# A fused chunk-selecting attention and ELU MLP on one core: selection moved to a [chunk, query] layout, persistent mask tiles, half-batch MLP with the ELU over three engines

## The chip, the cores and the metric

The kernel runs on one core of one Trainium2 chip. The metric is the device time of one execution in microseconds (us), as the median of several runs. Lower is better.

## The reference, cut to what matters

```python
# q, k, v: [4 batches, 8 heads, 768 positions, 64]; chunks of 32 keys, 24 chunks a head
k_min = np.min(k_chunks, axis=3); k_max = np.max(k_chunks, axis=3)
ub = np.sum(np.maximum(q*k_min, q*k_max), axis=-1)       # bound of each query against each chunk
ub = np.where(causal, ub, -1e9)
top_chunks = np.argsort(ub, axis=-1)[..., -6:]           # the 6 best chunks of each query
mask = sel & (pos[:, None] >= pos[None, :])
attn = softmax(where(mask, q @ k.T / 8, -1e9))           # shortened
x = (attn @ v) transposed to [3072 tokens, 512]          # shortened
h = x @ w_in                                             # w_in [512, 2048]
g = np.where(h > 0.0, h, np.exp(np.minimum(h, 0.0)) - 1.0)   # ELU
return g @ w_out                                         # w_out [2048, 512]
```

The work is done by head pairs: 4 batches with 4 pairs each give 16 pairs, called 0 to 15. A batch's MLP can start when its four pairs are done. The mask does not appear as a separate step in the score matmul: 24 extra rows of the stationary operand hold -40000 where a key belongs to a chunk, and 24 extra rows of the moving operand hold 1 where the query did *not* select that chunk. The score matmul of a pair therefore cannot start until its selection is known.

## The kernel before

Both weight matrices are asked for on the GpSimd queue as the last item of the set-up. For each pair, ScalarE copies the transposed queries out of PSUM, VectorE builds the operands, TensorE computes the bound in [query, chunk] layout, VectorE finds the sixth largest, TensorE transposes the selection, and VectorE copies it into the operand.

```python
psT = ... bufs=4, PSUM   # transposes, bounds
psS = ... bufs=3, PSUM   # scores and, under another name (psM = psS), all MLP results
psO = ... bufs=1, PSUM
# ... constants by GpSimd ...
w_in_sb = wpool.tile([P, DMODEL // P, DFF], BF16, name="w_in_sb")
nc.gpsimd.dma_start(out=w_in_sb, in_=moe_w_in.rearrange("(k p) f -> p k f", p=P))
w_out_sb = wpool.tile([P, DFF // P, DMODEL], BF16, name="w_out_sb")
nc.gpsimd.dma_start(out=w_out_sb, in_=moe_w_out.rearrange("(k p) f -> p k f", p=P))
# ...
# phase_b1, set-up of a pair
        nc.vector.tensor_copy(out=lhsA[64:P, :], in_=econst[64:P, :])      # three constant blocks
        nc.vector.tensor_copy(out=lhsB[0:64, :], in_=econst[0:64, :])      # copied anew for every pair
        nc.vector.tensor_copy(out=rhsA[64:P, :], in_=zconst[64:P, :])
        # ... q transposed by TensorE; 8 ScalarE copies of it, two of them Abs ...
        # ... k transposed; ScalarE copies it to KTf ...
        nc.vector.tensor_copy(out=lhsA[0:64, :], in_=KTf[0:64, :])
        nc.vector.tensor_copy(out=lhsB[64:128, :], in_=KTf[64:128, :])
        nc.vector.tensor_copy(out=vext[:, :, :, 0:D], in_=v_pair)
        # ... kmid = kmax + kmin, krad = kmax - kmin, per head block ...
# phase_b2, the bound of 128 queries at a time against 2 x 24 chunks, in fp32
        for qi, qt in enumerate(range(1, NQT)):
            nc.tensor.matmul(ub_ps[:, qi, :], lhsT=QTf[:, 128 * qt:128 * (qt + 1)], rhs=kmidBD,
                             start=True, stop=False)
            nc.tensor.matmul(ub_ps[:, qi, :], lhsT=absQTf[:, 128 * qt:128 * (qt + 1)], rhs=kradBD,
                             start=False, stop=True)
        # ... top six, comparison, 6 transposes of the selection ...
        nc.vector.tensor_copy(out=rhsB[0:64, 0:512], in_=selps0[0:64, :])
        nc.vector.tensor_copy(out=rhsA[64:88, 0:512], in_=selps0[64:88, :])
        # ...
# phase_d, MLP of a batch: 16 blocks of 128 hidden units x 768 tokens
            for hw, tc0, tw in ((hw0, 0, 512), (hw1, 512, 256)):
                nc.scalar.activation(out=e_sb[:, 0:tw], in_=hw, func=AF.Exp)
                nc.vector.tensor_scalar(out=t_sb[:, 0:tw], in0=e_sb[:, 0:tw], scalar1=1.0,
                                        scalar2=1.0, op0=AOT.min, op1=AOT.subtract)
                nc.vector.tensor_tensor(out=gT[:, fc, tc0:tc0 + tw], in0=t_sb[:, 0:tw],
                                        in1=hw, op=AOT.max)
```

The softmax here doesn't subtract the row's maximum and nothing guards it: scores larger than these inputs give would overflow.

Of the kernel before, what the change touches and what calls it, by code (L numbers as in the profile page):

```python
# [9 lines left out]
AOT = mybir.AluOpType  # L11
AF = mybir.ActivationFunctionType
F32 = mybir.dt.float32
# [10 lines left out]
NTOK = B * S  # L24
# [3 lines left out]
NQT = S // P  # L28
MASKNEG = -40000.0
CAUSNEG = -1.0e9  # L30

NPAIR = H // 2


@with_exitstack
def kernel(
# [8 lines left out]
    dev_pairs=None,  # L45
    dev_mlp=None,
    dev_dump=None,
# [3 lines left out]
    const = ctx.enter_context(tc.tile_pool(name="const", bufs=1))  # L51
    wpool = ctx.enter_context(tc.tile_pool(name="wpool", bufs=1))
    xtpool = ctx.enter_context(tc.tile_pool(name="xtpool", bufs=8))
    gtpool = ctx.enter_context(tc.tile_pool(name="gtpool", bufs=1))
    ldpool = ctx.enter_context(tc.tile_pool(name="ldpool", bufs=3))
    tspool = ctx.enter_context(tc.tile_pool(name="tspool", bufs=3))
    bigpool = ctx.enter_context(tc.tile_pool(name="bigpool", bufs=4))
    smpool = ctx.enter_context(tc.tile_pool(name="smpool", bufs=3))
    selpool = ctx.enter_context(tc.tile_pool(name="selpool", bufs=4))
    ptpool = ctx.enter_context(tc.tile_pool(name="ptpool", bufs=18))  # L60
    opool = ctx.enter_context(tc.tile_pool(name="opool", bufs=3))
    mlppool = ctx.enter_context(tc.tile_pool(name="mlppool", bufs=2))
    psT = ctx.enter_context(tc.tile_pool(name="psT", bufs=4, space=bass.MemoryType.PSUM))
    psS = ctx.enter_context(tc.tile_pool(name="psS", bufs=3, space=bass.MemoryType.PSUM))
    psO = ctx.enter_context(tc.tile_pool(name="psO", bufs=1, space=bass.MemoryType.PSUM))
    psM = psS
# [6 lines left out]
    nc.gpsimd.tensor_copy(out=ident_b, in_=ident_f)  # L73

    tri01 = const.tile([P, P], BF16, name="tri01")
    tri_tmp = const.tile([P, P], F32, name="tri_tmp")
    nc.gpsimd.memset(tri_tmp, 1.0)
    nc.gpsimd.affine_select(out=tri_tmp, in_=tri_tmp, compare_op=AOT.is_ge,
                            fill=0.0, base=0, pattern=[[1, P]], channel_multiplier=-1)
    nc.gpsimd.tensor_copy(out=tri01, in_=tri_tmp)  # L80

    e24_tmp = const.tile([P, S], F32, name="e24_tmp")
    nc.gpsimd.memset(e24_tmp, MASKNEG)
    for r0, cnt in ((0, 64), (64, 64)):
        nc.gpsimd.affine_select(out=e24_tmp[r0:r0 + cnt], in_=e24_tmp[r0:r0 + cnt],
                                compare_op=AOT.is_ge, fill=0.0, base=0,
                                pattern=[[1, S]], channel_multiplier=-32)
        nc.gpsimd.affine_select(out=e24_tmp[r0:r0 + cnt], in_=e24_tmp[r0:r0 + cnt],
                                compare_op=AOT.is_ge, fill=0.0, base=31,
                                pattern=[[-1, S]], channel_multiplier=32)  # L90
    econst = const.tile([P, S], BF16, name="econst")
    nc.gpsimd.tensor_copy(out=econst, in_=e24_tmp)
    zconst = const.tile([P, S], BF16, name="zconst")
    nc.gpsimd.memset(zconst, 0.0)

    causal_sel = const.tile([P, NQT, 2, NCH], F32, name="causal_sel")
    nc.gpsimd.memset(causal_sel, 0.0)
    for j in range(4):
        nc.gpsimd.affine_select(out=causal_sel[32 * j:32 * (j + 1)],
                                in_=causal_sel[32 * j:32 * (j + 1)],  # L100
                                compare_op=AOT.is_ge, fill=CAUSNEG, base=j,
                                pattern=[[4, NQT], [0, 2], [-1, NCH]], channel_multiplier=0)

    w_in_sb = wpool.tile([P, DMODEL // P, DFF], BF16, name="w_in_sb")
    nc.gpsimd.dma_start(out=w_in_sb, in_=moe_w_in.rearrange("(k p) f -> p k f", p=P))
    w_out_sb = wpool.tile([P, DFF // P, DMODEL], BF16, name="w_out_sb")
    nc.gpsimd.dma_start(out=w_out_sb, in_=moe_w_out.rearrange("(k p) f -> p k f", p=P))

    pairs = [(b, r) for b in range(B) for r in range(NPAIR)]
    if dev_pairs is not None:  # L110
        pairs = dev_pairs
    mlp_batches = list(range(B))
    if dev_mlp is not None:
        mlp_batches = dev_mlp

    xT = {}

    def phase_a(b, r):
        q_pair = ldpool.tile([P, NQT, 2, D], F32, name="q_pair")
        k_pair = ldpool.tile([P, NQT, 2, D], F32, name="k_pair")  # L120
        v_pair = ldpool.tile([P, NQT, 2, D], F32, name="v_pair")
        for hidx in range(2):
            hh = 2 * r + hidx
            nc.sync.dma_start(out=q_pair[:, :, hidx, :],
                              in_=q[b, hh].rearrange("(n p) d -> p n d", p=P))
            nc.sync.dma_start(out=k_pair[:, :, hidx, :],
                              in_=k[b, hh].rearrange("(n p) d -> p n d", p=P))
            nc.sync.dma_start(out=v_pair[:, :, hidx, :],
                              in_=v[b, hh].rearrange("(n p) d -> p n d", p=P))
        return (q_pair, k_pair, v_pair)  # L130

    def phase_b1(b, r, lds, resd):
        q_pair, k_pair, v_pair = lds
        lhsA = bigpool.tile([P, S], BF16, name="lhsA")
        lhsB = bigpool.tile([P, S], BF16, name="lhsB")
        rhsA = bigpool.tile([P, S], BF16, name="rhsA")
        rhsB = bigpool.tile([P, S], BF16, name="rhsB")
        nc.vector.tensor_copy(out=lhsA[64:P, :], in_=econst[64:P, :])
        nc.vector.tensor_copy(out=lhsB[0:64, :], in_=econst[0:64, :])
        nc.vector.tensor_copy(out=rhsA[64:P, :], in_=zconst[64:P, :])  # L140
        psQ0 = psT.tile([P, 512], F32, name="psQ0", tag="ps")
        psQ1 = psT.tile([P, 256], F32, name="psQ1", tag="ps")
        for n in range(NQT):
            src_q = q_pair[:, n, :, :]
            if n < 4:
                nc.tensor.transpose(psQ0[:, 128 * n:128 * (n + 1)], src_q, ident_f)
            else:
                nc.tensor.transpose(psQ1[:, 128 * (n - 4):128 * (n - 3)], src_q, ident_f)
        QTf = tspool.tile([P, S], F32, name="QTf")
        nc.scalar.activation(out=QTf[:, 0:512], in_=psQ0, func=AF.Copy, scale=0.5)  # L150
        nc.scalar.activation(out=QTf[:, 512:768], in_=psQ1, func=AF.Copy, scale=0.5)
        nc.scalar.activation(out=rhsA[0:64, 0:512], in_=psQ0[0:64, :], func=AF.Copy)
        nc.scalar.activation(out=rhsB[64:128, 0:512], in_=psQ0[64:128, :], func=AF.Copy)
        nc.scalar.activation(out=rhsA[0:64, 512:768], in_=psQ1[0:64, :], func=AF.Copy)
        nc.scalar.activation(out=rhsB[64:128, 512:768], in_=psQ1[64:128, :], func=AF.Copy)
        absQTf = tspool.tile([P, S], F32, name="absQTf")
        nc.scalar.activation(out=absQTf[:, 0:512], in_=psQ0, func=AF.Abs, scale=0.5)
        nc.scalar.activation(out=absQTf[:, 512:768], in_=psQ1, func=AF.Abs, scale=0.5)
        yield

        psK0 = psT.tile([P, 512], F32, name="psK0", tag="ps")
        psK1 = psT.tile([P, 256], F32, name="psK1", tag="ps")
        for n in range(NQT):
            src_k = k_pair[:, n, :, :]
            if n < 4:
                nc.tensor.transpose(psK0[:, 128 * n:128 * (n + 1)], src_k, ident_f)
            else:
                nc.tensor.transpose(psK1[:, 128 * (n - 4):128 * (n - 3)], src_k, ident_f)
        KTf = tspool.tile([P, S], F32, name="KTf")
        nc.scalar.activation(out=KTf[:, 0:512], in_=psK0, func=AF.Copy)  # L170
        nc.scalar.activation(out=KTf[:, 512:768], in_=psK1, func=AF.Copy)
        nc.vector.tensor_copy(out=lhsA[0:64, :], in_=KTf[0:64, :])  # L172
        nc.vector.tensor_copy(out=lhsB[64:128, :], in_=KTf[64:128, :])  # L173
        vext = selpool.tile([P, NQT, 2, D + 1], BF16, name="vext")
        nc.gpsimd.memset(vext[:, :, :, D:D + 1], 1.0)
        nc.vector.tensor_copy(out=vext[:, :, :, 0:D], in_=v_pair)  # L176
        kv = KTf[:, :].rearrange("p (c w) -> p c w", c=NCH)
# [18 lines left out]
                         rhsB=rhsB, vext=vext, kmidBD=kmidBD, kradBD=kradBD))  # L196

    def phase_b2(b, r, st):
        QTf = st["QTf"]
        absQTf = st["absQTf"]  # L200
        kmidBD = st["kmidBD"]
        kradBD = st["kradBD"]
# [257 lines left out]
```

## Time and profile before

| | before |
|---|---|
| time, median (lowest to highest of 3 runs) | 464.08 us (463.63 to 464.13) |
| span of the profiled run, mean granted TensorE clock | 461.3 us, 0.941 |
| first softmax exp | 51.3 us |
| pairs 0 to 3 (little else runs), first exp to the end of pair 3 | 57.7 us |

The page of the profile opens with the busy time of each engine, then cuts the span into 40 slices of 11.5 us; each digit is the busy share in tenths (the row of TensorE is shown), and PEclk is the clock that the throttle granted to TensorE.

```profile
span 461.3 us, 7376 instructions
PE 351.4 (76%) x2534; PEld 219.5 (48%) x2560; DVE 313.3 (68%) x1064; ACT 221.1 (48%) x513; POOL 26.4 (6%) x104
...
PE   3411986678569999778569999697478999878896
...
PEclk9999997798899999888899999977999999989999
```

No engine is full. In the first four slices (46 us) TensorE does 3, 4, 1 and 1 tenths. What ended its waits is listed by the view of waits (us in total, times, longest us):

```profile
PE h_ps L335 <- DVE gT L343: 22.9, 22, 3.5
PE sps L273 <- DVE rhsA L238: 21.7, 9, 3.3
PE selps_302 L236 <- DVE selv L227: 15.0, 1, 15.0
PE ub_ps L208 <- DVE kmidBD L188: 11.4, 2, 6.6
```

The four longest waits all end with VectorE: for the last ELU pass, which frees the MLP's PSUM buffer, for the mask rows that VectorE copies, and for the selection and its bound at the start. The timeline of the start (start us, us, engine, instruction) shows what VectorE itself stood behind:

```profile
10.81 0.93 POOL L105 DMA_DIRECT2D w_in_sb<-in_moe_w_in_dram  x1
...
11.74 1.29 POOL L107 DMA_DIRECT2D w_out_sb<-in_moe_w_out_dram  x1
...
12.47 9.45 SPq L128 DMA_DIRECT2D v_pair<-in_v_dram  x1
...
37.12 0.56 DVE L176 CAST vext<-v_pair 128x768 bf16<-128x768 f32 x1 [18.22 <-DMA v_pair<-in_v_dram]
...
51.30 1.08 ACT L276 ACTIVATE pt<-sps 128x512 bf16<-128x512 f32 x2 [6.51 <-PE sps L273]
```

The weights are asked for at 10.8 and 11.7 us. From then on the sync engine's issues stretch (9.45 us for one), and VectorE stands 18.2 us for one load of v. The first exp runs at 51.3 us.

In the MLP's first half alone, near the end, TensorE repeats a pattern; two blocks of 768 tokens lie between 429.25 and 432.81 us, 3.56 us for 2 x 3072 = 6144 columns:

```profile
429.25 0.60 PE L335 MATMUL h_ps<-xt,w_in_sb 128*128 128x256 bf16 x4 [0.31 <-DVE gT L343]
...
432.81 0.60 PE L335 MATMUL h_ps<-xt,w_in_sb 128*128 128x256 bf16 x4 [0.31 <-DVE gT L343]
```

The bound matmuls are fp32, and the trace records two passes for each: 160 matmuls leave 320 records. Eight passes lie between 63.95 and 64.85 us, about 0.11 us each:

```profile
63.95 0.39 PE L210 MATMUL ub_ps<-kradBD,absQTf 128*128 128x48 f32 x2
...
64.85 0.39 PE L210 MATMUL ub_ps<-kradBD,absQTf 128*128 128x48 f32 x2
```

### The profile page before, as it was taken

The numbers are of one execution on the slowest core, as the hardware profiler recorded it, in microseconds if no ns is written. First come the engines' busy times: TensorE is split into PE (matmuls) and PEld (weight loads), VectorE is DVE, ScalarE is ACT, GpSimd is POOL, SyncE is SP. The second block draws the span as 40 slices with busy tenths as digits, with TensorE's granted clock in tenths as the row PEclk, the third lists the DMA queues.
The fourth block names the chain that finished last, engine by engine and source line by source line (L and its number), as shares of the span: only waits on it lengthen the run. The fifth ranks groups of instructions, "written<-read, shape, count | busy, mean of one in ns | idle before, by whom it ended". The sixth has DMA issues, their size and how long they took to land.

```text
span 461.3 us, 7376 instructions
## 1 busy us (share of the span) xinstructions
PE 351.4 (76%) x2534; PEld 219.5 (48%) x2560; DVE 313.3 (68%) x1064; ACT 221.1 (48%) x513; POOL 26.4 (6%) x104
## 2 busy tenths in 40 slices
PE   3411986678569999778569999697478999878896
PEld 3301764556246445566236444575245644644442
DVE  3605688877958927877968916777968935769921
ACT  4303585576267207765267306773365505745500
POOL 9400000001000000000000000000000000000000
PEclk9999997798899999888899999977999999989999
DMA  9999342343003211442202211300000021000011
GB/s 219 213 195 257 90 96 64 89 102 85 19 2 69 58 68 48 104 102 59 47 1 68 59 68 47 70 1 1 0 1 1 2 86 52 2 0 1 0 70 68
DMA packets 81348, 29.83 MB, mean 65 GB/s; under 512 B 75680, under 2 KB 77728, under 8 KB 81312
## 3 DMA queue, kind: packets, MB, share of 16 engines
q1 hardware_dynamic: 78720, 25.17, 22.0%
q0 software_dynamic: 2592, 4.19, 5.0%
q8 instruction: 20, 0.33, 0.3%
q14 instruction: 16, 0.13, 0.1%
HBM read 27.26 MB, written 6.29 MB: 73 GB/s over the span
## 4 chain that ended last, share of the span: by engine, by line
PE 51%; DVE 30%; ACT 9%; issue 4%; SPq 4%; DMA 1%; DVEq 0%
PE mo_ps L349 18%; PE h_ps L333 8%; ACT pt L276 6%; PE sps L273 6%; DVE gT L343 5%; PE h_ps L335 5%; PE ub_ps L210 4%; PE ub_ps L208 4%; DVE t_sb L341 3%; PE o_ps L291 3%; ACT e_sb L339 3%; DVE kmax L180 3%; DVE kmin L181 2%; DVE lhsA L172 2%; DVE lhsB L173 1%
## 5 line engine op out<-in xcount | busy, mean ns | idle before, releaser
L276 ACT ACTIVATE pt<-sps 128x384 bf16<-128x384 f32 (+2 forms) x224 | 93.6, 508 | 113.2 <-PE sps L273 111.8
L339 ACT ACTIVATE e_sb<-h_ps 128x512 f32<-128x512 f32 (+1 forms) x128 | 61.1, 491 | 64.8 <-PE h_ps L333 35.5
L349 PE MATMUL mo_ps<-w_out_sb,gT 128*128 128x512 bf16 x376 | 83.1, 379 | 0.4
L333 PE MATMUL h_ps<-xt,w_in_sb 128*128 128x512 bf16 x238 | 71.8, 404 | 6.2 <-ACT pt L276 2.8
L343 DVE TENSOR_TENSOR gT<-t_sb,h_ps 128x512 bf16<-128x512 f32 (+1 forms) x128 | 66.7, 548 | 1.2
L335 PE MATMUL h_ps<-xt,w_in_sb 128*128 128x256 bf16 x256 | 46.1, 285 | 24.8 <-DVE gT L343 22.9
L273 PE MATMUL sps<-rhsA,lhsA 128*128 128x384 bf16 x144 | 41.7, 328 | 24.1 <-DVE rhsA L238 21.7
L349 PEld LDWEIGHTS <-gT 128*128 128x128 bf16 x384 | 37.6, 98 | 44.4
L341 DVE TENSOR_SCALAR t_sb<-e_sb 128x512 f32<-128x512 f32 (+1 forms) x128 | 43.7, 359 | 19.3 <-ACT e_sb L339 17.3
L352 DVE COPY o_sb<-mo_ps 128x512 f32<-128x512 f32 x24 | 16.6, 690 | 51.3 <-PE mo_ps L349 51.3
L273 PE MATMUL sps<-rhsB,lhsB 128*128 128x384 bf16 x144 | 41.2, 322 | 10.8 <-ACT pt L276 10.2
L335 PEld LDWEIGHTS <-w_in_sb 128*128 128x128 bf16 x256 | 25.9, 102 | 45.1 <-issue 38.5
L291 PEld LDWEIGHTS <-pt 128*128 128x128 bf16 x672 | 32.7, 107 | 22.9 <-DVE pt L280 14.3
L291 PE MATMUL o_ps<-vext,pt 128*128 128x65 bf16 x672 | 38.7, 207 | 3.3 <-DVE pt L280 2.8
L208 PE MATMUL ub_ps<-kmidBD,QTf 128*128 128x48 f32 x160 | 32.0, 284 | 11.4 <-DVE kmidBD L188 11.4
L333 PEld LDWEIGHTS <-w_in_sb 128*128 128x128 bf16 x256 | 25.9, 104 | 30.1 <-issue 16.2
L280 DVE TENSOR_TENSOR pt<-pt,tri_107 128x128 bf16<-128x128 bf16 x192 | 31.3, 220 | 5.1 <-ACT pt L276 3.8
L208 PEld LDWEIGHTS ub_ps<-kmidBD,QTf 128*128 128x128 f32 x160 | 27.2, 209 | 13.1 <-issue 12.2
L210 PE MATMUL ub_ps<-kradBD,absQTf 128*128 128x48 f32 x160 | 33.2, 291 | 0.0
L273 PEld LDWEIGHTS <-lhsA 128*128 128x128 bf16 x144 | 14.1, 106 | 35.8 <-DVE rhsA L238 23.8
L176 DVE CAST vext<-v_pair 128x768 bf16<-128x768 f32 x16 | 8.9, 558 | 28.4 <-DMA v_pair<-in_v_dram 28.2
L210 PEld LDWEIGHTS ub_ps<-kradBD,absQTf 128*128 128x128 f32 x160 | 26.7, 209 | 0.0
(538 smaller groups left out, 400.4 us busy)
## 6 DMA issues: line engine op xcount, KB each, us to landing
q_pair<-in_q_dram SPq DMA_DIRECT2D x32, 192.0 KB, 3.2
k_pair<-in_k_dram SPq DMA_DIRECT2D x32, 192.0 KB, 3.1
v_pair<-in_v_dram SPq DMA_DIRECT2D x32, 192.0 KB, 3.2
out_dram<-o_sb SPq DMA_DIRECT2D x24, 256.0 KB, 2.0
w_in_sb<-in_moe_w_in_dram POOLq DMA_DIRECT2D x1, 2048.0 KB, 14.0
w_out_sb<-in_moe_w_out_dram POOLq DMA_DIRECT2D x1, 2048.0 KB, 26.4
```

The source lines that it names most:

```text
L208: nc.tensor.matmul(ub_ps[:, qi, :], lhsT=QTf[:, 128 * qt:128 * (qt + 1)], rhs=kmidBD, start=True, stop=False)
L210: nc.tensor.matmul(ub_ps[:, qi, :], lhsT=absQTf[:, 128 * qt:128 * (qt + 1)], rhs=kradBD, start=False, stop=True)
L273: nc.tensor.matmul(sps[:, pc:pc + w], lhsT=lhs_of[hd][:, 128 * kb:128 * (kb + 1)], rhs=rhs_of[hd][:, c0:c0 + w], start=True, stop=True)
L276: nc.scalar.activation(out=pt[:, 0:wtot], in_=sps[:, 0:wtot], func=AF.Exp, scale=SCALE)
L280: nc.vector.tensor_tensor(out=pt[:, pc:pc + 128], in0=pt[:, pc:pc + 128], in1=tri01, op=AOT.mult)
L291: nc.tensor.matmul(o3_ps[:, hd, qi, :], lhsT=pt[:, off:off + 128], rhs=vext[:, kb, hd, :], start=(kb == 0), stop=(kb == qt))
L333: nc.tensor.matmul(hw0, lhsT=wblk, rhs=xT[(b, kk)][:, 0:512], start=(kk == 0), stop=(kk == DMODEL // P - 1))
L335: nc.tensor.matmul(hw1, lhsT=wblk, rhs=xT[(b, kk)][:, 512:768], start=(kk == 0), stop=(kk == DMODEL // P - 1))
L339: nc.scalar.activation(out=e_sb[:, 0:tw], in_=hw, func=AF.Exp)
L341: nc.vector.tensor_scalar(out=t_sb[:, 0:tw], in0=e_sb[:, 0:tw], scalar1=1.0, scalar2=1.0, op0=AOT.min, op1=AOT.subtract)
L343: nc.vector.tensor_tensor(out=gT[:, fc, tc0:tc0 + tw], in0=t_sb[:, 0:tw], in1=hw, op=AOT.max)
L349: nc.tensor.matmul(o_ps, lhsT=gT[:, fc, 128 * tt:128 * (tt + 1)], rhs=w_out_sb[:, fc, :], start=(fc == 0), stop=(fc == DFF // P - 1))
```

## The change

The intent: take VectorE, which ended the longest waits, out of the way of TensorE. The bound is computed transposed, with the chunks as the stationary side and 288 queries moving, two pairs side by side in the two column halves of the array. Its formula changes with it: instead of q and |q| against the middle and the width of a chunk's range, it is q against the chunk's minimum plus max(q, 0), called Qrl in the traces, against maximum less minimum. The first 192 queries see at most six chunks and are left out, so 576 queries remain. VectorE's 32x32 block transpose turns it for the top-six search and back, and four small DMAs put the selection into the operands of two pairs; no TensorE transpose and no VectorE copy remains. The constant blocks are written once into four persistent sets. The MLP works on half batches of 384 tokens, and its middle ELU pass goes to GpSimd. Loads of q and k are issued before the set-up, and the weights after the first preparation. The core of the diff (the whole file is rewritten; cuts are marked by `...`, and the comments are added here):

```diff
-    psT = ctx.enter_context(tc.tile_pool(name="psT", bufs=4, space=bass.MemoryType.PSUM))
-    psS = ctx.enter_context(tc.tile_pool(name="psS", bufs=3, space=bass.MemoryType.PSUM))
-    psM = psS
+    psT = pool("psT", 2, space=bass.MemoryType.PSUM)
+    psS = pool("psS", 2, space=bass.MemoryType.PSUM)
+    psM = pool("psM", 3, space=bass.MemoryType.PSUM)
 ...
+    lds = {t: load(t) for t in range(2)}                  # q and k first, before the constants
 ...
+    for s in range(NSET):                                 # once, not per pair
+        nc.vector.tensor_copy(out=lhsA[s][64:P, :],
+                              in_=econst[64:P].rearrange("p c w -> p (c w)"))
 ...
+            nc.scalar.activation(out=lhsA[s][0:64, ts], in_=ps[0:64, :], func=AF.Copy)    # K
+            nc.scalar.activation(out=lhsB[s][64:P, ts], in_=ps[64:P, :], func=AF.Copy)
 ...
+    def select(g):                                        # for two pairs at once
+        for u in range(2):
+            ub = psT.tile([P, HQ], F32, name="ub", tag="ps")
+            for w in range(2):
+                for j in range(2):
+                    t = 2 * g + j
+                    nc.tensor.matmul(ub[64 * j:64 * j + 64, :], lhsT=kst[t % NSET][:, w, :],
+                                     rhs=qf[t][w][:, HQ * u:HQ * (u + 1)],
+                                     start=(w == 0), stop=(w == 1))
+            nc.vector.transpose(out=ubT[:, HB * u:HB * (u + 1), :].rearrange("p b c -> p (b c)"),
+                                in_=ub)
 ...
+        nc.vector.transpose(out=selT, in_=sb[:, :, :].rearrange("p b c -> p (b c)"))
+        for j in range(2):
+            s = (2 * g + j) % NSET
+            nc.sync.dma_start(out=rhsA[s][64:64 + NCH, Q0:S], in_=selT[64 * j:64 * j + NCH, :])
+            nc.sync.dma_start(out=rhsB[s][0:NCH, Q0:S], in_=selT[64 * j + 32:64 * j + 32 + NCH, :])
 ...
-                nc.vector.tensor_scalar(out=t_sb[:, 0:tw], in0=e_sb[:, 0:tw], scalar1=1.0,
-                                        scalar2=1.0, op0=AOT.min, op1=AOT.subtract)
-                nc.vector.tensor_tensor(out=gT[:, fc, tc0:tc0 + tw], in0=t_sb[:, 0:tw],
-                                        in1=hw, op=AOT.max)
+            nc.gpsimd.tensor_scalar(out=m_sb, in0=e_sb, scalar1=-1.0, scalar2=1.0,
+                                    op0=AOT.add, op1=AOT.mult)
+            nc.vector.scalar_tensor_tensor(out=gT[:, fc, :], in0=hw, scalar=0.0, in1=m_sb,
+                                           op0=AOT.max, op1=AOT.min)
 ...
+    prep_group(0)
+    load_w_in()
+    select(0)
+    prep_group(1)
+    load_w_out()
+    for g in range(ng):
+        attend(2 * g)
+        if g + 1 < ng:
+            select(g + 1)
+        attend(2 * g + 1)
+        if g + 2 < ng:
+            prep_group(g + 2)
+        if g % 2 == 1 and g >= 3:
+            for hf in range(2):
+                mlp((g - 3) // 2, hf)
```

## The prediction

> **What bounds the kernel now.** Span 461 us; no engine is full: TensorE 351 us (76%), VectorE 313 (68%), ScalarE 221 (48%), GpSimd 26 (the page's busy table). The chain of waits is 51% TensorE, 30% VectorE, 9% ScalarE. The stretches read:
> - Start: the first softmax exp runs near 49 us. TensorE is busy only 12 us in the first 46. Both weight matrices (8.4 MB at 215 GB/s) are asked for at 11 us; the SP queue's issues then stretch from 0.6 to 3-9 us, and pair 2's loads arrive late (timeline).
> - Attention alone (50-112 us): 15-16 us a pair. VectorE is 76-82% busy; the score matmuls wait 3.3 us a pair for the mask rows that VectorE copies into rhs; the granted clock falls to 0.73.
> - MLP, first half alone (425-437 us): 3.55 us per two blocks, where the matmuls need 2.6 at full clock: TensorE waits for ScalarE then two VectorE passes to free three PSUM buffers.
> - MLP, second half: 96 matmuls at 217 ns, 20.9 us a batch, pure TensorE. Untouched.
>
> **What changes, costed from the trace.**
> - ELU: the min/subtract pass (43.7 us VectorE) goes to GpSimd as 128 passes of 128x384. GpSimd's casts took 280 ns (128 wide) and 1030 (768): about 0.6 us each, 75 us total, an estimate. The last pass stays: 0.55 us x 128 = 70 us against 66.7.
> - Setup copies a pair (econst, zconst, lhs casts, vext, mask rows, block-diagonal builds): about 4 us of VectorE a pair disappear (persistent tiles, cast on the v DMA, ScalarE copies). The 192 triangle products become 64 larger ones. MAX8 only 160 -> 144.
> - Together VectorE falls from 313 to about 215 us. ScalarE stays near 225 (Q/absQ/KTf copies replaced by half-width ones).
> - TensorE: 320 fp32 bound matmuls at 110 ns (weight-load bound, 36 us) become 64 of 288 columns; 0.25-0.5 us each, 15-31 us. 96 selection transposes vanish (5 us). Hidden-layer matmuls 83 us either way. Pipelined work at full clock: about 309 -> 290 us. So TensorE hardly shrinks; what goes is its waiting.
> - Start: q/k first, weights after the first preps; attention should begin near 25 us, not 49. The mask now goes by four small DMAs on the SP queue behind loads.
>
> **Sum.** About 25 us start. Pairs 0-7 are mostly attention in the new instruction order: ScalarE 9.9 us a pair, TensorE 7.7 at full clock; say 12 us: 96 us, hiding some 11 us of MLP. Left: eight pairs and the MLPs, about 218 us TensorE at full clock; at 0.95 clock and 6% stalls 243. Tail 4. Total about 368; I say 370. TensorE should then be near 85% busy.
>
> The Trainium skill, "TensorE: Matmul & The Clock Gate", part 1, says idle TensorE windows lower its clock; this trace agrees (0.73 at 69-92 us, 1.00 when dense). Denser work should raise the mean above 0.941. "GPSIMD Engine Reference", section 1, says GpSimd shares SBUF interfaces with VectorE and contends with two-SBUF-input or two-port passes; no number here shows it.
>
> **What would show each step.** GpSimd m_sb mean near 0.6 us; VectorE total 205-230; first exp by 25-28 us; bound-matmul pitch under 0.5 us; MLP-only blocks near 0.8 us (three PSUM buffers, chain 2.4 us); mean clock at or over 0.95; last MLP's second half unchanged at 10.4 us per half-batch.
>
> **What would make it wrong.** GpSimd passes over 1 us, lengthening the PSUM release; v DMAs waiting in GpSimd's in-order queue ahead of ELU passes; mask DMAs held behind loads at each group; only two score and two transpose PSUM buffers (three and four before) starving the attention stage; ScalarE, unrelieved, pacing longer than assumed. Better: fp32 bound matmuls run in parallel column halves, stalls vanish: 345.

## More of the kernel before

The page counts time before the first clock record as full clock; in this trace the records begin only at 56.1 us, so the first four digits of PEclk and most of the fifth are not measured.

## The result

| | before | after |
|---|---|---|
| time, median (lowest to highest of 4 runs) | 464.11 us (463.63 to 465.49) | 396.31 us (395.87 to 396.63) |
| ratio, 95% interval | | 0.852 (0.850 to 0.855) |
| profiled span, mean clock as printed | 461.3 us, 0.941 | 394.6 us, 0.930 |
| first softmax exp | 51.3 us | 49.6 us |
| first exp to the end of pair 3 | 57.7 us | 52.5 us |
| first exp to the end of the span | 410.0 us | 344.9 us |

A ratio is the mean time of one kernel's runs over that of the other's runs of the same rounds, so it is not quite the ratio of the medians that are quoted. An unchanged copy of the kernel after, run later, gave 396.16 us and 0.852 again.

The page of the kernel after, the same lines:

```profile
span 394.6 us, 6477 instructions
PE 317.5 (80%) x2272; PEld 175.1 (44%) x2272; DVE 205.0 (52%) x594; ACT 226.5 (57%) x489; POOL 116.2 (29%) x244
...
PE   1562068678869869999998788999999988979886
...
PEclk9995559959998989999999699999999999999999
```

VectorE fell from 313.3 to 205.0 us. TensorE fell from 351.4 to 317.5 us and is busier (80%). Its idle time, span less busy time, fell from 109.9 to 77.1 us. So of the 66.7 us of span, 33.9 us are work that TensorE no longer does, and 32.8 us are waiting that is gone. In the first 49 us its idle time hardly moved (34.2 us before, 33.1 after). After those 49 us it was 75.8 us before and is 44.0 after. So almost the whole gain lies after the start. The waits of TensorE, after:

```profile
PE sps L243 <- DMA rhsA_119<-selT: 15.4, 1, 15.4
PE h_ps L295 <- DVE gT L303: 11.5, 28, 0.8
PE sps L243 <- ACT pt L246: 11.2, 18, 2.3
PE psQ L182 <- ACT lhsB_118 L169: 7.3, 5, 3.8
```

The waits for VectorE's mask rows and selection are gone. A single wait of 15.4 us for the first mask DMA has taken their place, and ScalarE now stands where VectorE stood. The start, in the timeline after:

```profile
10.93 0.68 POOL L145 DMA_DIRECT2D w_in_sb<-in_moe_w_in_dram  x1
...
28.02 0.77 DVE L214 STREAM_TRANSPOSE selT<-selb_171 128x576 bf16<-128x576 bf16 x1
...
31.59 9.38 SPq L85 DMA_DIRECT2D q_pair<-in_q_dram  x2
...
41.07 5.13 SPq L82 DMA_DIRECT2D k_pair<-in_k_dram  x2
...
46.30 0.86 SPq L217 DMA_DIRECT2D rhsA_119<-selT  x1
...
49.62 0.60 ACT L246 ACTIVATE pt<-sps 128x512 bf16<-128x512 f32 x1 [16.95 <-PE sps L243]
```

The selection of pairs 0 and 1 is complete at 28.8 us. The sync engine sends it at 46.3 us; until then it stands in the issue of later loads of q and k. The first weight is still asked for at 10.93 us, against 10.81 before: issuing the weights "after the first preps" moved nothing, because no instruction made the GpSimd queue wait for anything.

The MLP's first half alone, at the end of the run, and the output half that follows it:

```profile
371.81 2.11 PE L295 MATMUL h_ps<-xt,w_in_sb 128*128 128x384 bf16 x12 [0.53 <-DVE gT L303]
374.44 2.11 PE L295 MATMUL h_ps<-xt,w_in_sb 128*128 128x384 bf16 x12 [0.53 <-DVE gT L303]
...
380.37 10.52 PE L308 MATMUL o_ps<-w_out_sb,gT 128*128 128x512 bf16 x48
```

Three blocks take 2.63 us, 0.88 us a block of 384 tokens. Before, two blocks of 768 took 3.56 us, or 0.89 us per 384: the same. Three blocks and then a stop of 0.53 us is the mark of three PSUM buffers. The bound matmuls, after:

```profile
91.73 0.41 PE L200 MATMUL ub<-QTf,kst_121 128*64 128x288 f32 x1
91.74 0.41 PE L200 MATMUL ub<-QTf,kst_127 128*64 128x288 f32 x1
91.97 0.41 PE L200 MATMUL ub<-Qrl,kst_121 128*64 128x288 f32 x1
91.98 0.41 PE L200 MATMUL ub<-Qrl,kst_127 128*64 128x288 f32 x1
```

The passes of the two pairs (kst_121 and kst_127) start within 10 ns of each other, and the next couple starts 0.24 us later. The kernel has 64 such matmuls of two passes each, that is 64 couples of passes: an estimate at full clock is 64 x 0.243 us = 15.6 us of TensorE, where 320 passes at 0.111 us took 35.5, so 20 us less. By busy time, in which the 33.9 us are counted, these matmuls fell from 42.4 to 20.7 us, and the 96 selection transposes, 11.7 us before, are gone. Both overlap with other matmuls: with the two groups left out, TensorE is busy 309.2 us before and 297.9 after, so about 11 of the 33.9 us lie elsewhere.

### The profile page after: what moved, and what is told of

It reads as the page before. It is cut to its first block, busy times and chain, and to the rows that moved or that the text cites. A ratio compares the mean times of both kernels' runs of the same rounds, so it can differ in the third digit from the quotient of the medians.

```text
span 394.6 us, 6477 instructions
## 1 busy us (share of the span) xinstructions
PE 317.5 (80%) x2272; PEld 175.1 (44%) x2272; DVE 205.0 (52%) x594; ACT 226.5 (57%) x489; POOL 116.2 (29%) x244
## 4 chain that ended last, share of the span: by engine, by line
issue 30%; PE 24%; ACT 18%; POOL 16%; DVE 8%; SPq 3%; DMA 1%; POOLq 0%; ACTq 0%
POOL m_sb L301 13%; PE o_ps L308 9%; ACT pt L246 5%; PE sps L243 4%; PE ub L200 3%; DVE gT L303 2%; PE h_ps L295 2%; SPq L85 2%; PE psK L162 2%; PE psQ L182 2%; ACT QTf L187 1%; SPq L82 1%; ACT e_sb L299 1%; ACT rhsB_120 L189 1%; ACT lhsB_118 L169 1%
## 5 line engine op out<-in xcount | busy, mean ns | idle before, releaser
L295 PE MATMUL h_ps<-xt,w_in_sb 128*128 128x384 bf16 x512 | 105.3, 327 | 12.1 <-DVE gT L303 11.5
L301 POOL TENSOR_SCALAR m_sb<-e_sb 128x384 f32<-128x384 f32 x128 | 65.6, 516 | 155.2 <-ACT e_sb L299 143.8
L246 ACT ACTIVATE pt<-sps 128x384 bf16<-128x384 f32 (+1 forms) x160 | 80.4, 534 | 53.4 <-PE sps L243 51.5
L303 DVE SCALAR_TENSOR_TENSOR gT<-h_ps,m_sb 128x384 bf16<-128x384 f32 x128 | 70.4, 554 | 41.4 <-POOL m_sb L301 38.1
L308 PE MATMUL o_ps<-w_out_sb,gT 128*128 128x512 bf16 x384 | 88.1, 379 | 0.0
L299 ACT ACTIVATE e_sb<-h_ps 128x384 f32<-128x384 f32 x128 | 62.3, 496 | 40.4 <-PE h_ps L295 38.6
L182 PE MATMUL psQ<-ident_f,q_pair 128*128 128x128 f32 x96 | 21.0, 338 | 17.3 <-ACT lhsB_118 L169 7.3
L162 PE MATMUL psK<-ident_f,k_pair 128*128 128x128 f32 x96 | 19.2, 317 | 11.2 <-DMA k_pair<-in_k_dram 4.6
L243 PE MATMUL sps<-rhsA_119,lhsA_117 128*128 128x384 bf16 (+2 forms) x36 | 9.9, 315 | 18.4 <-DMA rhsA_119<-selT 15.4
L255 DVE TENSOR_TENSOR pt<-pt,tri_168 128x512 bf16<-128x512 bf16 x32 | 13.5, 421 | 13.4 <-ACT pt L246 13.4
L249 ACT ACTIVATE pt<-sps 128x512 bf16<-128x512 f32 x32 | 19.3, 604 | 1.4 <-PE sps L243 1.3
L285 DVE COPY xt<-pxt 128x384 bf16<-128x384 bf16 x32 | 11.3, 352 | 16.2 <-PE pxt L284 15.8
L165 DVE TENSOR_REDUCE kmm<-psK 128x12 f32<-128x384 f32 x32 | 17.6, 549 | 3.9 <-PE psK L162 3.4
L166 DVE TENSOR_REDUCE kmm<-psK 128x12 f32<-128x384 f32 x32 | 17.4, 545 | 0.0
```

What stands on the lines that cost most here:

```text
L162: nc.tensor.transpose(ps[:, P * n:P * (n + 1)], k_pair[:, 3 * h + n], ident_f)
L165: nc.vector.tensor_reduce(out=kmm[:, 0, cs], in_=pv, axis=AX.X, op=AOT.min)
L182: nc.tensor.transpose(ps[:, P * n:P * (n + 1)], q_pair[:, 3 * h + n], ident_f)
L243: nc.tensor.matmul(sps[:, o + pc:o + pc + w], lhsT=lhs[hd][:, P * kb:P * (kb + 1)], rhs=rhs[hd][:, c0:c0 + w], start=True, stop=True)
L246: nc.scalar.activation(out=pt[:, hd, 0:wtot], in_=sps[:, 0:wtot], func=AF.Exp, scale=SCALE)
L249: nc.scalar.activation(out=pt[:, :, 0:256], in_=sps[:, :].rearrange("p (h w) -> p h w", h=2), func=AF.Exp, scale=SCALE)
```

## The experiments

After the comparison there were three places where the predicted time had been missed or could be doubted, each with rival readings:

- **The start.** Either the weights' traffic on the shared DMA engines holds everything behind it; or the fault is the sync queue alone, where the mask stands behind loads; or the start hardly matters, because later stages take the time back.
- **The attention stage.** Either ScalarE paces it (67 us busy out of 86 in a stretch of six pairs), or TensorE's other waits do.
- **The MLP.** Either the three PSUM buffers limit a block to 0.88 us, or the last VectorE pass does; and the pass on GpSimd either matters or does not.

The quoted expectations name their theories by letters; the text here names them in words. The runs came in three calls, with the kernel before at 466.6, 465.1 and 464.9 us (medians); the ratios allow for that.

### Mask DMAs from ScalarE's queue: e1_mask_actq

```diff
-            nc.sync.dma_start(out=rhsA[s][64:64 + NCH, Q0:S], in_=selT[64 * j:64 * j + NCH, :])
-            nc.sync.dma_start(out=rhsB[s][0:NCH, Q0:S], in_=selT[64 * j + 32:64 * j + 32 + NCH, :])
+            nc.scalar.dma_start(out=rhsA[s][64:64 + NCH, Q0:S], in_=selT[64 * j:64 * j + NCH, :])
+            nc.scalar.dma_start(out=rhsB[s][0:NCH, Q0:S], in_=selT[64 * j + 32:64 * j + 32 + NCH, :])
```

> Only the queue that issues the four mask transfers of a group changes: ScalarE's instead of SyncE's. In the changed kernel the first mask is computed at 28.8 us and issued at 46.3, the first exp runs at 49.6. Theory A (the weights' traffic holds every transfer: the mask also has to wait until earlier loads, whose completion slots it reuses, have landed): the issue stays over 40 us, the first exp over 43, total 390 to 400 us. Rival B (the mask only stands behind load instructions in SyncE's program order): issue near 29, first exp 31 to 34, total 378 to 384.

Measured: 409.97 us, ratio 0.880 (0.876 to 0.884): by the medians 13.7 us worse than the kernel after. That is beyond the expected 390 to 400. ScalarE's timeline of this run:

```profile
31.01 1.32 ACTq L217 DMA_DIRECT2D rhsA<-selT  x1
40.97 0.73 ACTq L218 DMA_DIRECT2D rhsB<-selT  x1
...
48.59 0.48 ACT L168 ACTIVATE lhsA<-psK 64x384 bf16<-64x384 f32 x1 [19.88 <-DMA rhsA<-selT]
```

The first of the four goes out at 31.0 us, but the next three only at 41.0, 45.1 and 47.8 us. ScalarE does no other work for 19.9 us meanwhile, and the first exp runs at 49.97 us, no earlier. So the queue alone was not the fault: the mask transfers are held on another queue too, and the first of them takes 5.6 us to land, against 2.1 in e5_gate_two_steps below, where no weights are under way. The Trainium skill, "DMA: Bandwidth & Descriptors", section "Issuing engines are not separate DMA queues", says that transfers started by different engines run on the same 16 DMA engines and interleave, and that several issuing engines save only issue time; this run agrees. The packed trace of this run shows what holds the other three: each waits for a load of k or q whose completion counter it takes over. Those loads were issued at 25.7, 27.7 and 35.8 us and complete at 40.95, 45.05 and 47.79 us, each 0.02 to 0.03 us before the mask transfer goes out. Why the run lost 13.7 us, beyond a start that was no later, was not settled. Pair 7 ended at 166.6 us here against 158.8, and ScalarE, standing in order at each group's mask transfers, is the likely reason; that is argued, not shown.

### Weights held until the first selection: e2_weights_gated

A one-element copy from the selection into the weight tile ahead of each weight DMA makes the DMA wait.

```diff
-    def load_w_in():
+    def load_w_in(g):
         for kk in range(NKK):
+            nc.vector.tensor_copy(out=w_in_sb[0:1, kk, 0:1], in_=g)
             nc.gpsimd.dma_start(out=w_in_sb[:, kk, :], in_=moe_w_in[P * kk:P * (kk + 1), :])
 # ... the same in load_w_out; select() returns selT[0:1, 0:1] ...
-    load_w_in()
-    select(0)
+    g0 = select(0)
+    load_w_in(g0)
     prep_group(1)
-    load_w_out()
+    load_w_out(g0)
```

> Both weight loads are made to wait for the first selection by a one-element write into their tiles; nothing else changes, mask still on SyncE's queue. Theory A (weights' traffic in the first 46 us is what holds the mask): first mask issued by 30 us, first exp 31 to 35, and since TensorE is nearly idle there the total falls by about as much, 14 to 18 us: 378 to 383. Rival B (program order of the queue alone): first mask still over 40 us, total over 390. Rival C (the start is made up for later, because the MLP then waits for weights): first exp early, total over 390.

Measured: 391.15 us, ratio 0.839 (0.835 to 0.844), outside the range of the first reading. The total is the one that the third reading gave (over 390), but its reason, an MLP that waits for weights, is not what the trace shows. The timeline of this run, the first and the second selection:

```profile
28.59 0.88 SPq L219 DMA_DIRECT2D rhsA<-selT  x1
...
33.96 0.60 ACT L249 ACTIVATE pt<-sps 128x512 bf16<-128x512 f32 x1 [1.42 <-PE sps L246]
...
53.15 0.77 DVE L216 STREAM_TRANSPOSE selT<-selb 128x576 bf16<-128x576 bf16 x1
...
63.28 0.75 SPq L219 DMA_DIRECT2D rhsA<-selT  x1
...
65.52 0.61 PE L246 MATMUL sps<-rhsA,lhsA 128*128 128x384 bf16 x2 [9.28 <-DMA rhsA<-selT]
```

The first mask now goes out at 28.6 us and the first exp runs at 34.0 us, 15.7 us earlier than in the kernel after. But the same thing then happens one group later: the second selection is ready at 53.9 us and is sent at 63.3, behind loads that are slow beside the weights. The cure moved the jam instead of removing it. So the cause of the start was hit (the weights), but the expected gain was taken back by a new wait, which can be named.

### Weights held in two steps: e5_gate_two_steps

The gates of e2, but w_in waits for the second selection and w_out for the third; the early calls are removed.

```diff
-            select(g + 1)
+            gg = select(g + 1)
+            if g == 0:
+                load_w_in(gg)
+            if g == 1:
+                load_w_out(gg)
```

> As e2, but the first weight matrix waits for the second selection and the other for the third. In e2 the first exp came at 34.0 us instead of 49.6, yet pair 1 ended only 6 us earlier than before, because the second group's mask, ready at 53.9, was issued at 63.3. Theory A2 (in e2 the weights' traffic merely held the next mask; nothing else ate the 10 us): second mask issued within 2 us of being ready, pairs 1, 3, 5 and 7 end 13 to 16 us earlier than in the changed kernel, total 379 to 384. Rival C (a hidden limit of the first pairs, such as the clock or the loads of q and k, gives it back anyway): total 388 to 392.

Measured: 380.92 us, ratio 0.819 (0.817 to 0.821), 15.2 us better than the unchanged kernel, and in the expected range. The first and the second selection in this run:

```profile
27.90 0.88 SPq L219 DMA_DIRECT2D rhsA<-selT  x1
...
51.58 0.77 DVE L216 STREAM_TRANSPOSE selT<-selb 128x576 bf16<-128x576 bf16 x1
...
52.37 0.76 SPq L219 DMA_DIRECT2D rhsA<-selT  x1
```

Both are sent at once. (While w_in is loaded, the four transfers of the second still take 2.0 to 6.3 us to land.) The first exp runs at 32.9 us, 16.7 us earlier, pairs 1, 3, 5 and 7 end 14.2 to 16.2 us earlier, and 15.2 us reach the end. That settles the start: the weights' traffic held the mask. It also settles that the start is on the critical path.

### The same cure in the kernel before: b1_before_gated

```diff
-    nc.gpsimd.dma_start(out=w_in_sb, in_=moe_w_in.rearrange("(k p) f -> p k f", p=P))
-    nc.gpsimd.dma_start(out=w_out_sb, in_=moe_w_out.rearrange("(k p) f -> p k f", p=P))
+    def load_weights(g):
+        nc.vector.tensor_copy(out=w_in_sb[64:65, 0, 0:1], in_=g)
+        nc.vector.tensor_copy(out=w_out_sb[64:65, 0, 0:1], in_=g)
+        # ... the same two DMAs ...
 # ... at the end of the loop's step t == -1 ...
+            load_weights(st[0]["rhsA"][64:65, S - 1:S])
```

> The kernel BEFORE with its two weight loads held until the first mask is in place (a one-element write); its mask goes by copies on VectorE, not by transfers. In the kernel before, the weights were asked for at 10.8 us, in the changed one at 10.9: the reordering moved nothing. Theory A (the weights' traffic, not the program's order of prologue work, sets the start in both kernels): first exp near 28-33 us instead of 49, total 10 to 18 us less: 446 to 454. Rival (start of the old kernel limited by its own prologue): under 4 us.

Measured: 449.11 us, ratio 0.967 (0.963 to 0.970), in the expected range; the first exp runs at 34.8 us instead of 51.3 (28 to 33 was expected). The kernel before paid about the same, 16 us, for the same reason. The change neither caused nor removed this.

### K copies back on VectorE: e6_kcopy_dve

```diff
-            nc.scalar.activation(out=lhsA[s][0:64, ts], in_=ps[0:64, :], func=AF.Copy)
-            nc.scalar.activation(out=lhsB[s][64:P, ts], in_=ps[64:P, :], func=AF.Copy)
+            nc.vector.tensor_copy(out=lhsA[s][0:64, ts], in_=ps[0:64, :])
+            nc.vector.tensor_copy(out=lhsB[s][64:P, ts], in_=ps[64:P, :])
```

> The four copies of K a pair go from ScalarE to VectorE. ScalarE falls by about 31 us to 195, VectorE rises to about 238. Theory G (ScalarE, busy 78% of pairs 2 to 7, paces the attention stretch at 14.3 us a pair): 1 us or more a pair less, total 385 to 390. Rival H (that stretch is paced by waits among engines at two-deep PSUM buffers, so no single engine's load matters): within 1% of the control.

Measured: 382.79 us, ratio 0.824 (0.822 to 0.826), 13.4 us better than the unchanged kernel. The direction fits ScalarE as the pacer; the gain is 2 us over the expected range. The stretch from 73 to 159 us (window, us, busy PE, PEld, DVE, ACT, POOL with counts, granted clock, DMA share, GB/s), first the kernel after:

```profile
73.00:159.00 86.00, 69.07 (x591) 40.11 (x590) 52.57 (x176) 67.16 (x147) 23.78 (x52) 0.90 0.48 74
```

and this run:

```profile
73.00:159.00 86.00, 71.04 (x636) 42.38 (x636) 72.36 (x217) 58.91 (x132) 25.45 (x60) 0.98 0.56 91
```

ScalarE is less busy (67.2 to 58.9 us) although more work passes through: TensorE has 636 records for 591. VectorE rises from 52.6 to 72.4 us and can bear it. TensorE's waits for the exp in that stretch fall from 5.8 to 2.3 us, and pairs 2 to 7 take 12.7 us each instead of 14.4. The granted clock rose from 0.90 to 0.98, and how much of the gain came that way was not separated. So the load on ScalarE held back the attention stage of the kernel after. The copies also free the two PSUM buffers of the transposes, and the run does not tell ScalarE's busy time from its late release of these buffers. Taking the K copies from VectorE had been one item too many.

### The ELU pass back on VectorE: e4_elu_dve

```diff
-            nc.gpsimd.tensor_scalar(out=m_sb, in0=e_sb, scalar1=-1.0, scalar2=1.0,
+            nc.vector.tensor_scalar(out=m_sb, in0=e_sb, scalar1=-1.0, scalar2=1.0,
```

> The exp(h)-1 pass goes back from GpSimd to VectorE, 128 passes of 128x384. Theory D (the split bought nothing in the MLP-only stretches, which are paced by three PSUM buffers and the chain exp, minus one, min, at 0.88 us a block both with the split and, as 3.55 us per four 384-column equivalents, before it): VectorE grows by about 46 us to 250, MLP-only blocks 0.85 to 0.95 us, total 394 to 402. Rival E (the split is what frees VectorE, and is worth its 46 us of passes in large part): total over 415.

Measured: 393.79 us, ratio 0.845 (0.841 to 0.849), just below the expected range. VectorE is busy 239.3 us instead of 205.0, and a block of the MLP alone takes 0.86 us instead of 0.88. So the split over three engines gave VectorE 34 us back, and in this kernel, with three PSUM buffers, they bought no time. The 0.7 points by which this run is even the better one come from different chips, and were not pursued.

### Five PSUM buffers for the last MLP: e8_tail_psum

In the last batch no attention runs beside the MLP, so two of five hidden blocks borrow the two idle score buffers.

```diff
-            h_ps = psM.tile([P, 512], F32, name="h_ps", tag="psm")
+            if b == B - 1 and fc % 5 >= 3:
+                h_ps = psS.tile([P, 512], F32, name="sps")
+            else:
+                h_ps = psM.tile([P, 512], F32, name="h_ps", tag="psm")
```

> For the last batch only, two of every five hidden blocks take their PSUM tile from the score pool, which is idle by then: five buffers instead of three. Theory D (the chain of 2.64 us over three buffers paces MLP-only blocks): the last batch's blocks fall from 0.88 to 0.66-0.70 us, 32 blocks, total 5 to 7 us less: 389 to 391. Rival F (the blocks are paced by an engine's throughput or a hand-over, not by the count of buffers): 0.85 us or more, total 395 to 397.

Measured: 389.19 us, ratio 0.835 (0.831 to 0.839), as expected. TensorE in the last hidden half of this run:

```profile
362.68 2.11 PE L298 MATMUL h_ps<-xt,w_in_sb 128*128 128x384 bf16 x12
364.63 1.46 PE L298 MATMUL sps<-xt,w_in_sb 128*128 128x384 bf16 x8
365.93 2.11 PE L298 MATMUL h_ps<-xt,w_in_sb 128*128 128x384 bf16 x12
```

Five blocks take 3.25 us, 0.65 us each, with no stop between them. The number of buffers set the 0.88 us, not TensorE.

### Five buffers and the pass on VectorE: e14_tail_dve

The edits of the last two runs together.

> e8 and e4 together: five PSUM buffers for the last batch and the minus-one pass on VectorE. If with VectorE doing both passes the blocks are paced by VectorE (0.36 + 0.55 us), the last batch stays at 0.86 us a block and the total equals e4's within 1 us, where e8 with GpSimd reached 0.65 us. If the buffers were the limit in e4 too: 0.65-0.70 us and 6 us less than e4.

Measured: 386.26 us, ratio 0.832 (0.828 to 0.835). I had expected VectorE, with both passes, to become the limit at about 0.86 us a block. That fell: the last 16 blocks lie between 359.28 and 370.04 us, 0.67 us each. The total is 7.5 us under e4's, by the medians. The trace shows why: VectorE's last ELU passes end 0.74 us apart (361.61 to 372.73 us for the 16 blocks), so VectorE is slower than TensorE, falls about 1 us behind within the half batch, and finishes under the output matmuls that follow. So it is the buffer count that set the 0.86 to 0.88 us, whichever engine does the middle pass; with five buffers and a longer run of blocks VectorE would be the next limit.

### Order of the bound matmuls: e9_ub_serial

```diff
-            for w in range(2):
-                for j in range(2):
+            for j in range(2):
+                for w in range(2):
                     t = 2 * g + j
```

> The order of the bound matmuls only: both of one pair, then both of the other, instead of alternating; the two pairs write different column halves of the array. In the changed kernel two such passes start within 10 ns and the 128 half-passes (two for each fp32 matmul) take 20.7 us of TensorE. If neighbours in different halves really run at once: busy of these matmuls rises to 27-32 us and the total by 0 to 8 us. If they do not: busy stays at 20-22 us and the total within 1 us of 396.

Measured: 397.26 us, ratio 0.855 (0.852 to 0.859), the same as the kernel after; busy time of these matmuls 21.1 us against 20.7. The timeline:

```profile
91.08 0.71 PE L200 MATMUL ub<-QTf,kst 128*64 128x288 f32 x4
91.62 0.66 PE L200 MATMUL ub<-Qrl,kst 128*64 128x288 f32 x4
```

In the kernel's text, the first pair's Qrl matmul now comes before the second pair's QTf matmul. In the trace the four QTf passes of both pairs still run first. That the new order reached the chip shows in the offsets: most couples start 13 to 14 ns apart in this run, and 6 to 8 ns apart in the kernel after and its control. So the edit did not make the two pairs run one after the other, and the expected ranges of busy time decide nothing. The two column halves of the array keep their own order and run beside each other, whatever the order between them. The Trainium skill, "TensorEngine Tiling (Array Packing)", section "Key Properties", says that "Tiles operate independently: Different tiles can execute LdWeights and Matmul in parallel"; both traces agree.

### Three cures together: c2_three_cures

The edits of e5 and e6, and the five buffers for the last three half batches.

> Changed kernel with three cures: weights held back in two steps (alone worth 15.2 us), K copies on VectorE (13.4 us), and five PSUM buffers for the hidden blocks of the last three half-batches (7 us for two of them). If they are independent: 396.2 - 15.2 - 13.4 - 10.5 = 357, so 353 to 362. If they overlap (an earlier start is waited away at TensorE): 365 to 372.

Measured: 366.34 us (364.70 to 367.88), ratio 0.788 (0.785 to 0.792), the best version and correct. It lies in the range of the second reading: the cures overlap. Simple addition would have given 357 us. The cure of the tail arrived in full: from pair 15 to the end of the span takes 74.8 us instead of 85.4. The two cures of the front overlap: pair 7 ends 19.4 us earlier than in the kernel after, where they gave 16.1 and 9.9 us apart. One line of the waits of TensorE in this run is new:

```profile
PE psQ L184 <- DVE lhsB L171: 8.1, 2, 6.8
```

During the first 35 us VectorE, which fills the persistent tiles and now also copies K, is busy 25 us, and TensorE waits for its K copy. This makes the first exp 2.8 us later than in e5 (35.7 against 32.9), but pair 1 ends at the same time in both (58.6 and 58.4 us). The 6.6 us that are missing from the sum lie after it: pairs 2 and 3 take 28.8 us here and 24.8 in e6. In this run w_in and w_out are loaded beside them (53 to 67 and 83 to 96 us); whether that is the cause was not tried.

### One shared PSUM pool: c4_one_psum_pool

The edits of e5 and e6, with the score and MLP pools merged into one of five buffers.

```diff
-    psS = pool("psS", 2, space=bass.MemoryType.PSUM)
-    psM = pool("psM", 3, space=bass.MemoryType.PSUM)
+    psM = pool("psM", 5, space=bass.MemoryType.PSUM)
```

> As c2, but score and MLP tiles share one pool of five PSUM buffers throughout instead of two and three with borrowing at the end. If two score buffers starve the attention stretch: 3 to 8 us under c2. If MLP blocks that fill the shared pool hold up attention: over c2.

Measured: 386.61 us, ratio 0.831 (0.829 to 0.834), 20 us worse than c2_three_cures. Up to pair 7, where only attention runs, it is 7 us ahead (132.0 against 139.4 us); pair 8 then ends at 189.3 against 181.2, and pair 15 at 301.7 against 288.0. Pairs 2 to 7 take 12.2 us each, against 13.5 in c2_three_cures: two score buffers did hold back the attention stage, a risk that the prediction had named. Once the MLP runs beside attention, it seems to hold back the scores that the next MLP needs; the order of events fits this, and it was not tested apart. The split into 2 and 3 in the change is therefore worth keeping; lending buffers only where attention is over is better than sharing them throughout.

### The control: after_again

> The changed kernel unaltered, as the control of this chip: 395 to 399 us, ratio to the kernel before 0.852.

Measured: 396.16 us, ratio 0.852 (0.850 to 0.853), as before. The differences above of 7 us and more are well over what repeats vary.

## Why the prediction was right or wrong

**The direction was right, the mechanism in part, and the size was 26 us short.** I predicted 370 us; measured were 396.3. VectorE's work fell as costed and TensorE's waits for its mask rows and selection went; the start did not move. The sum that I wrote was 25 (start) + 96 (pairs 0 to 7 at 12 us) + 243 (the rest) + 4 (tail) = 368. The same parts of the trace after are:

| part | predicted | measured | difference |
|---|---|---|---|
| start, to the first exp | 25 | 49.6 | +24.6 |
| pairs 0 to 7 | 96 (12 a pair) | 109.2 (13.65 a pair) | +13.2 |
| the rest and the tail (to the time of 396.3) | 247 | 237.5 | -9.5 |
| sum | 368 | 396.3 | +28.3 |

**The step that failed** is the one that I wrote as "Start: q/k first, weights after the first preps; attention should begin near 25 us, not 49". It began at 49.6. The program text put the weights later, but GpSimd waits for nothing and asked for them at 10.93 us, as before. The weights, 8.4 MB in memory, were among the loads, which moved 191 GB/s in the first 49 us by the profile's count; the last packet of the weights ended at 45.8 us, and the first mask transfer of 27 KB, ready at 28.8 us, went out at 46.3. e1 shows that another queue is no cure, e5 that holding back the weights is, and b1 that the kernel before had the same fault. I had listed "mask DMAs held behind loads at each group" among what could go wrong, but left its cost out of the sum. The 25 us were too low besides: in e5, with no jam, the first exp runs at 32.9 us, since the preparation and selection of the first pairs themselves last until 27.9. So about 17 of the 24.6 us are the jam and 8 are an underestimated preparation.

**The second term that was mis-sized** is "say 12 us" a pair; it took 13.65. I had costed ScalarE at 9.9 us a pair and then allowed 2 for stalls. ScalarE's load held this stage back, as e6 shows: without the K copies pairs 2 to 7 take 12.7 us instead of 14.4. I had named this risk ("ScalarE, unrelieved, pacing longer than assumed"), and that of the two score buffers, which c4 shows.

**The rest came out 9.5 us better.** I took a clock of 0.95 there and 6% of stalls; from 159 us on the trace grants 0.98 to 0.99, and TensorE's idle share is 9%. That this term offset part of the other two was luck. Over the whole run the printed clock is 0.930, not "at or over 0.95". The largest loss is at the start: from 39.5 to 59.2 us TensorE was busy 35% and the granted clock was 0.50, in the kernel after:

```profile
39.50:59.20 19.70, 6.97 (x37) 3.69 (x37) 2.29 (x6) 8.54 (x19) 0.00 (x0) 0.50 0.97 199
```

The Trainium skill, "TensorE: Matmul & The Clock Gate", Part 1 "What's actually happening", describes a gate that passes half of the clock pulses when TensorE has not been busy; this trace agrees. But the printed means, 0.941 before and 0.930 after, cannot be compared. The clock records begin at 56.1 us before and at 25.0 us after, and the time ahead of them is counted as full clock. In that time the fp32 transposes of q and k start 213 ns apart in both traces, which is their pitch in recorded stretches at half clock; at full clock it is 109 ns. With half clock put in there, an estimate from these numbers, the means are 0.88 before and 0.90 after: the clock rose, as predicted, and stayed under 0.95. The three cures together have 0.965 as printed and 0.93 by the same estimate.

**Right:**

- VectorE fell to 205.0 us (205 to 230 predicted), GpSimd's m_sb took 516 ns on average (about 0.6 us), and the output half stayed at 10.5 us per half batch (10.4).
- The MLP block alone was predicted near 0.8 us and took 0.88; that the three PSUM buffers set it was right (e8).
- The bound matmuls lie under 0.5 us. At 15.6 us in all they are at the low end of "15-31 us", since the column halves run side by side; I had kept that for the optimistic case.
- The GpSimd contention that I mentioned from the skill did not show in the GpSimd passes: m_sb took 502 ns at least, 512 at the median and 648 at most.

**Right for a wrong reason.** I gave the ELU split as one of the items that relieve VectorE, which it does. But e4 shows that the relief bought nothing. The gain after the start is TensorE's shorter work (15 to 20 us of it the bound matmuls, as their overlap with other matmuls is counted) and the end of its waits for VectorE's mask rows and selection, as the two lists of waits show. That is read from the two traces: no run undid the new selection or the persistent tiles alone, and how the 32.8 us of vanished waiting divide among the removed VectorE copies, the new PSUM pools and the half batches was not tried.

**Open:** why e1 lost so much beyond its start; whether the 0.7 points in favour of e4 are real; how much of e6's gain is clock; and what holds pairs 2 and 3 of c2_three_cures.

## What to carry to other kernels

Moving a large load later in the program text does not move it in time unless its engine has something to wait for: give it a real dependency, and release it in steps, or the jam only moves to the next small transfer. When work is taken from one engine, ask for each item which engine is last in that stage; here two items of the same rewrite (K copies to ScalarE, the ELU pass to GpSimd) were harmful or idle. If a loop stops regularly after as many blocks as there are buffers, count the buffers before speeding up the engines, and lend idle ones only where their owner has finished.

## What the Trainium skill lacked or had wrong

- "TensorE: Matmul & The Clock Gate", Part 3, says that matmuls are strictly in program order in start and end. In e9, whose changed order reached the chip (the couples' offset went from 6 to 8 ns to 13 to 14), four QTf passes of both pairs start from 91.08 us and the Qrl passes only from 91.62, although the first pair's Qrl matmul precedes the second pair's QTf matmul in the kernel's text. Between two column halves the order does not hold.
- The same page gives no time for an fp32 matmul. Here each leaves two records, called passes above; a pass with 288 moving columns takes 0.243 us at full clock, also with two column halves at work, and one with 48 moving columns 0.111 us.
- "DMA: Bandwidth & Descriptors" does not say how long a small transfer may wait behind loads that are slow beside a large one. Here a 27 KB mask waited from 28.8 to 46.3 us on the sync queue, and from 31.0 to 47.8 us for the last of four on ScalarE's.
- "GPSIMD Engine Reference" has rates per element but no time for a one-input pass with two scalars: 512 ns at the median for 128x384 in fp32.
- "Vector Engine (DVE) Microarchitecture Reference" gives a rate for VectorE's 32x32 block transpose, one element a cycle per lane, but no time for shapes like these. Here one took 768 ns for 128x576 in bf16, and 472 ns on average for 128x288 in fp32 out of PSUM.
